# x of two groups fetched from DRAM by chunk instead of whole, in a fused attention and mixture-of-experts kernel

## The chip, the cores and the metric

The kernel runs on one core of a Trainium2 chip. The metric is the device time of one execution in microseconds; lower is better. The core has five engines with an instruction stream each, all in order: PE (matmul; its weight loads are shown apart, as PEld), DVE and ACT (elementwise), POOL, and SP, which here issues most of the DMA transfers. An engine whose next instruction waits for something holds up all that is queued behind it.

## The reference

A linear recurrence with a complex decay per channel gives y, and y, with the heads side by side, is the input x of a dense mixture of four experts:

```python
a_re_n, a_im_n = a * (min(mag, 0.999) / (mag + 1e-6))      # complex decay, 48 channels a head
for t in range(768):
    S = a_n[t] * S + k[t] (outer) v[t]                      # complex state, 48x48, 4x8 heads
    y[t] = q[t] @ real(S)
x = y.transpose(0, 2, 1, 3).reshape(3072, 384)
p = probs / (probs.sum(-1) + 1e-9)
out = sum over 4 experts e of  p[:, e] * (relu(x @ w1[e]) @ w2[e])     # w1 384x1024, w2 1024x384
```

## The kernel before

The 3072 rows are cut into 12 groups of G = 256 columns (tokens), each of two chunks of C = 128. For a group the attention part takes A, Q and K (prefix products and norms on DVE and ACT), sends Q and K to DRAM and back in another layout (trips `q_d`, `k_d` into `Qst`, `Kst`), and per chunk makes scores (`sc`), values (`yp`) and the increment of the state (`dp`) on PE. ACT evicts the values of a chunk into its half of the tile y.

The first two experts run beside the attention: while group g - 1 goes through `moe1` (16 slices of the hidden width, in 8 steps k of two), `between(k)` fits in the pieces of the attention of group g. A step multiplies x by a slice of w1 into `ph`; ACT makes hh = relu(ph) and DVE hl = relu(ph) - hh, and the matmuls of w2 on hh and hl go into `po` one step later. Each number is carried as a high and a low part, so x is split too: `split_x` makes xh, a copy by ACT in a reduced type, and xl = x - xh by DVE. Whenever an expert is done, ACT scales `po` into acc (L649), which frees the PSUM bank. Behind the 12 groups a second stage (phb, pob) runs the other two experts.

How x comes from y depends on the group. In groups 0 to 2 (`g < XSEL`) PE turns y of each chunk into the layout of x (`turn_x`), and `split_x` gets two parts. In groups 3 to 11 y goes to DRAM in two transfers (`store_y`, L623, one for each half of the partitions) once both chunks are evicted, and `load_x` (L159) fetches it whole into the tile x, of which there is one; L166 copies and L168 subtracts all 768 elements of each partition at once. The load has to wait on SP until the stores have landed. In `between` the three pieces of a group's attention are taken at three steps in a row from `FIRST` on (steps 4, 5, 6 for groups three and four), and `split_x` is called at step 7, the last one.

The order of instructions on an engine is not the order of the code: a planner writes it from simulated times, with the program's order as priority, except where `behind` or `tc.keep_in_program_order` fixes it. The latter sets an instruction behind the one traced before it on its engine; the copies and subtractions of `split_x` are so set.

Of the kernel before, what the change touches and what calls it, by code (L numbers as in the profile page):

```python
# [8 lines left out]
F32 = mybir.dt.float32  # L9
# [6 lines left out]
B, H, S, D = 4, 8, 768, 48  # L16
# [3 lines left out]
P = 128  # L20
NJ = HD // P
C = 128
G = 256
# [11 lines left out]
IM = 64  # L35
# [23 lines left out]
XSEL = 3  # L59
FIRST = {1: 5, 2: 5, 3: 4, 4: 4, 5: 3, 6: 3}  # L60
STEP = {1: 4.2, 2: 4.2, 3: 4.2, 4: 4.2, 5: 4.2}
MORE = (1.9, 1.9, 0.5)
HALF = (2, 3, 4, 5)
HOFF = 96
WIDE = 32 + P + 48
DMA_SCRATCH = 4096
# [2 lines left out]
def fast_path(ctx, tc, qkP, aP, vP, probsP, w, out, flag):  # L69
    nc = tc.nc  # L70
    const = ctx.enter_context(tc.tile_pool(name="const", bufs=1))
    wpool = ctx.enter_context(tc.tile_pool(name="wpool", bufs=NF1))
    moe = ctx.enter_context(tc.tile_pool(name="moe", bufs=2))
# [29 lines left out]
    y_d = [dram.tile([HD, G], F32, name=f"y_d{g}") for g in range(NG)]  # L103
# [50 lines left out]
        wts[i] = (hi, lo)  # L154
        return last_pe if ps is not None else None

    def load_x(g):
        x = moe.tile([P, NJ, G], F32, tag="x", name=f"xa{g}", bufs=1)
        nc.sync.dma_start(x, y_d[g].rearrange("(j p) t -> p j t", p=P))  # L159
        return [(slice(0, G), x)]  # L160

    def split_x(g, parts):
        xh = moe.tile([P, NJ, G], F32R, tag="xh", name=f"xha{g}")
# [65 lines left out]
    with ExitStack() as c1:  # L229
# [29 lines left out]
        nc.gpsimd.memset(TA, 0.0)  # L259
        band = moe.tile([M, HOFF + P + IM], F32, tag="x", name="band", bufs=1)  # L260
        nc.gpsimd.memset(band, 0.0)
        for r0, base in ((0, HOFF), (IM, HOFF + D)):
            nc.gpsimd.affine_select(out=band[r0:r0 + D], in_=band[r0:r0 + D], pattern=[[-1, HOFF + P + IM]],
                                    compare_op=ALU.not_equal, fill=1.0, base=base, channel_multiplier=1)
# [190 lines left out]
        def trip(nm, X, dst, lo=0, hi=CG, prev=None):  # L455
            w = X.shape[-1] if hi == CG else C
            dt = dram.tile([2, HD, hi - lo, w], F32, name=nm)
            for c in range(2):
                sent = nc.sync.dma_start(dt[c].rearrange("(j p) n t -> p j n t", p=P),
                                         X[:, c].rearrange("p (j n) t -> p j n t", n=CG)[:, :, lo:hi, :w])  # L460
                if prev is not None:
                    behind(sent, prev)

            def back(prev=None):
                for c in range(2):
                    landed = nc.sync.dma_start(dst[c * IM:c * IM + D, :, lo:hi, :w],
                                               dt[c].rearrange("(h d) n t -> d h n t", d=D))
                    if prev is not None:
                        behind(landed, prev)
                return landed  # L470
            back.sent = sent
            return back

        def t_factors(g):
            Tr, Ti = Qst[0:D, :, CG - 1, C:], Qst[IM:M, :, CG - 1, C:]
            ins = nc.scalar.activation(TA[0:D], Tr, AF.Copy)
            tc.keep_in_program_order(ins)
            behind(ins, state["y", g, CG - 1 if g < NSEL else 0])
            tc.keep_in_program_order(nc.scalar.activation(TA[IM:M], Tr, AF.Copy))
            tc.keep_in_program_order(nc.scalar.activation(TB[IM:M], Ti, AF.Copy))  # L480
            tc.keep_in_program_order(nc.scalar.activation(TB[0:D], Ti, AF.Copy, scale=-1.0))
# [80 lines left out]
        def rotate(g):  # L562
            if (g + 1) % GB == 0:
                return
            Gt = state[g, CG]

            def bt(ap):
                return ap.broadcast_to([ap.shape[0], H, D])

            nc.vector.tensor_tensor(P2[0:D], Gt[IM:M], bt(TB[IM:M]), op=ALU.mult)  # L570
            nc.vector.tensor_tensor(P2[IM:M], Gt[0:D], bt(TB[0:D]), op=ALU.mult)
            nc.vector.tensor_tensor(Gt, Gt, bt(TA), op=ALU.mult)
            state["dve"] = nc.vector.tensor_tensor(Gt, Gt, P2, op=ALU.add)
            state[g + 1, 0] = Gt

        def turn_x(g, c, y):
            xp = ps_a.tile([P, NJ, C], F32, tag="pa", name=f"xp{g}_{c}")
            for j in range(NJ):
                ps = [p for p in range(HP) if -HOFF < 2 * D * p - P * j < P]
                for p in ps:  # L580
                    o = HOFF - (2 * D * p - P * j)
                    state["xp"] = nc.tensor.matmul(xp[:, j, :], band[:, o:o + P], y[:, p, c * C:(c + 1) * C],  # L582
                                                   start=(p == ps[0]), stop=(p == ps[-1]))
            return slice(c * C, (c + 1) * C), xp

        def near_attention(g, QK):
# [26 lines left out]
            xs.append(turn_x(g, 1, y))  # L613
            yield xs
            store_y(g, y)
            t_factors(g)
            inc1()
            rotate(g)

        def store_y(g, y):  # L620
            yv = y_d[g].rearrange("(p u d) t -> u d p t", u=2, d=D)
            for u in range(2):
                nc.sync.dma_start(yv[u], y[u * IM:u * IM + D])  # L623

        def attention(g, QK):
            y = small.tile([M, HP, G], F32, tag="y", name=f"y{g}")
            (turn0, _, inc0, sc0, val0), (turn1, _, inc1, sc1, val1) = (chunk(g, c, QK[1], y) for c in range(CG))
            turn0()
            inc0()
            yield sc0()  # L630
            val0()
            t_factors(g)
            xs = [turn_x(g, 0, y)] if g < XSEL else None
            yield sc1()
            val1()
            if g < XSEL:
                xs.append(turn_x(g, 1, y))
            store_y(g, y)
            x = xs or load_x(g)
            turn1()  # L640
            inc1()
            rotate(g)
            yield x

        def moe1(g, xh, xl, between=None, prev=None):
            def done(e, po):
# [37 lines left out]
        def front(g, A, qk):  # L684
# [36 lines left out]
            yield 3.0  # L721
            if g in HALF:
                qb = [trip(f"q_d{g}_{c}", Q, Qst, c, c + 1) for c in range(CG)]
# [10 lines left out]
            else:  # L734
# [5 lines left out]
                qb()  # L740
                last["q"] = kb()
            todo[g] = attention(g, (Q, K))

        x = {}
# [345 lines left out]
```

## Time and profile before

| | us |
|---|---|
| median of 3 runs | 1008.11 (1007.4 to 1008.57) |
| the profiled execution | 1010.09 |
| its span in the trace | 1008.3 |
| PE busy | 981.6 (97%) |
| weight loads busy | 921.5 (91%) |
| DVE busy | 590.3 (59%) |
| ACT busy | 363.6 (36%) |
| POOL busy | 35.6 (4%) |

Busy times are sums over one profiled execution. PE is the engine that is nearly always busy; DVE and ACT are averages over a first part, to about 520 us, in which DVE is nearly as busy as PE, and a second part in which both do little. Matmul ends are modelled, so a short idle time of PE is better judged together with the waits of its weight loads. Group three's x is copied at 196.5 us, group four's at 244.8.

### The profile page before, as it was taken

The numbers are of one execution on the slowest core, as the hardware profiler recorded it, in microseconds if no ns is written. First come the engines' busy times: TensorE is split into PE (matmuls) and PEld (weight loads), VectorE is DVE, ScalarE is ACT, GpSimd is POOL, SyncE is SP. The second block draws the span as 40 slices with busy tenths as digits, with TensorE's granted clock in tenths as the row PEclk, the third lists the DMA queues.
The fourth block names the chain that finished last, engine by engine and source line by source line (L and its number), as shares of the span: only waits on it lengthen the run. The fifth ranks groups of instructions, "written<-read, shape, count | busy, mean of one in ns | idle before, by whom it ended". The sixth has DMA issues, their size and how long they took to land.

```text
span 1008.3 us, 16256 instructions
## 1 busy us (share of the span) xinstructions
PE 981.6 (97%) x6618; PEld 921.5 (91%) x6618; DVE 590.3 (59%) x1228; ACT 363.6 (36%) x652; POOL 35.6 (4%) x66
## 2 busy tenths in 40 slices
PE   5899999999999999999999999999999999999997
PEld 3899998999999999999999999999999899989996
DVE  7889989898987989798942462232132322321221
ACT  7755525446364453636422352121111211211110
POOL 6030000000000000000000000000000000000000
PEclk9899999999999999999999999999999999999999
DMA  9584277384673836548161780020030110100001
GB/s 311 162 177 134 64 189 156 119 204 110 166 191 111 225 108 160 157 119 213 60 162 46 252 297 33 1 94 32 1 126 1 42 52 1 63 1 1 32 1 35
DMA packets 88676, 111.15 MB, mean 110 GB/s; under 512 B 5840, under 2 KB 72960, under 8 KB 88592
## 3 DMA queue, kind: packets, MB, share of 16 engines
q1 hardware_dynamic: 84016, 94.11, 33.4%
q0 software_dynamic: 4576, 15.91, 5.2%
q8 instruction: 54, 0.88, 0.4%
q14 instruction: 30, 0.25, 0.1%
HBM read 74.09 MB, written 35.90 MB: 109 GB/s over the span
## 4 chain that ended last, share of the span: by engine, by line
PE 85%; DVE 4%; DMA 4%; ACT 4%; issue 1%; SPq 0%; DVEq 0%; ACTq 0%
PE pob L862 20%; PE phb L849 20%; PE po L198 16%; PE ph L179 16%; PE sc L530 4%; PE dp L518 3%; PE yp L551 2%; PE yp L546 2%; PE ktp L500 1%; DMA q_d<-Q 1%; DMA y_d<-y 1%; DMA Kst<-k_d 1%; DMA xa<-y_d 1%; PE xp L582 1%; DVE Q L430 1%
## 5 line engine op out<-in xcount | busy, mean ns | idle before, releaser
L855 DVE SCALAR_TENSOR_TENSOR hlb<-phb,hhb 128x512 fp32r<-128x512 f32 x96 | 66.4, 691 | 270.6 <-ACT hhb L854 270.6
L854 ACT ACTIVATE hhb<-phb 128x512 fp32r<-128x512 f32 x96 | 57.4, 598 | 314.9 <-PE phb L849 299.6
L198 PE MATMUL po<-whi,hh 128*128 128x384 f32 x384 | 129.6, 339 | 1.1 <-ACT hh L188 1.1
L862 PE MATMUL pob<-wlo,hhb 128*128 128x384 f32 x384 | 129.2, 337 | 0.0
L198 PE MATMUL po<-wlo,hh 128*128 128x384 f32 x384 | 128.9, 336 | 0.0
L862 PE MATMUL pob<-whi,hhb 128*128 128x384 f32 x384 | 128.9, 336 | 0.0
L198 PE MATMUL po<-whi,hl 128*128 128x384 f32 x384 | 124.5, 339 | 0.7 <-DVE hl L189 0.6
L862 PE MATMUL pob<-whi,hlb 128*128 128x384 f32 x384 | 120.4, 336 | 0.0
L188 ACT ACTIVATE hh<-ph 128x512 fp32r<-128x512 f32 x96 | 57.2, 596 | 153.3 <-PE ph L179 151.0
L179 PE MATMUL ph<-xha,whi 128*128 128x256 f32 x576 | 103.8, 286 | 0.6 <-ACT xha L166 0.6
L179 PE MATMUL ph<-xha,wlo 128*128 128x256 f32 x576 | 101.5, 283 | 0.0
L179 PE MATMUL ph<-xla,whi 128*128 128x256 f32 x576 | 100.8, 284 | 0.4 <-DVE xla L168 0.4
L189 DVE SCALAR_TENSOR_TENSOR hl<-ph,hh 128x512 fp32r<-128x512 f32 x96 | 66.1, 689 | 49.5 <-ACT hh L188 48.9
L849 PE MATMUL phb<-xhb,whi 128*128 128x512 f32 x288 | 91.8, 392 | 0.0
L179 PEld LDWEIGHTS ph<-xha,whi 128*128 128x128 f32 x576 | 86.0, 190 | 1.8 <-issue 0.9
L179 PEld LDWEIGHTS ph<-xla,whi 128*128 128x128 f32 x576 | 82.5, 191 | 0.6 <-DVE xla L168 0.6
L179 PEld LDWEIGHTS ph<-xha,wlo 128*128 128x128 f32 x576 | 82.8, 190 | 0.2 <-issue 0.2
L849 PE MATMUL phb<-xlb,whi 128*128 128x512 f32 x288 | 82.7, 392 | 0.0
L849 PE MATMUL phb<-xhb,wlo 128*128 128x512 f32 x288 | 82.3, 393 | 0.0
L862 PEld LDWEIGHTS pob<-whi,hhb 128*128 128x128 f32 x384 | 72.1, 188 | 3.6
L862 PEld LDWEIGHTS pob<-wlo,hhb 128*128 128x128 f32 x384 | 72.1, 188 | 3.3
L198 PEld LDWEIGHTS po<-whi,hh 128*128 128x128 f32 x384 | 72.4, 189 | 1.8 <-ACT hh L188 1.3
(165 smaller groups left out, 1569.2 us busy)
## 6 DMA issues: line engine op xcount, KB each, us to landing
wst<-w SPq DMA_DIRECT2D x24, 384.0 KB, 5.5
qk<-qkP SPq DMA_DIRECT2D x24, 384.0 KB, 7.0
acc_d<-acc POOLq DMA_DIRECT2D x24, 384.0 KB, 3.6
prev<-acc_d SPq DMA_DIRECT2D x24, 384.0 KB, 5.0
A<-aP SPq DMA_DIRECT2D x22, 384.0 KB, 8.0
q_d<-Q SPq DMA_DIRECT2D x12, 387.0 KB, 4.2
Qst<-q_d SPq DMA_DIRECT2D x12, 387.0 KB, 5.9
v<-vP SPq DMA_DIRECT2D x24, 192.0 KB, 2.7
```

The costliest lines, as they stand in the source:

```text
L179: ins = nc.tensor.matmul(ph[:, u, :], wt[:, j * P:(j + 1) * P], xt[:, j, :], start=(n == 0), stop=(n == 3 * NJ - 1))
L188: wts["hh"] = nc.scalar.activation(hh, ph, AF.Relu)
L189: nc.vector.scalar_tensor_tensor(hl, ph, 0.0, hh, op0=ALU.max, op1=ALU.subtract)
L198: nc.tensor.matmul(po[t], ht[:, u, t * P:(t + 1) * P], wt[:, HD:], start=(i % FE == 0 and n == 0), stop=(i % FE == FE - 1 and n == 2))
L518: nc.tensor.matmul(d_ps[:, h, :], KT[:, h, :], vc[:, h * D:(h + 1) * D], start=True, stop=True)
L530: ins = nc.tensor.matmul(s_ps[:, h, :], Kc[:, hf * 4 + h, :], Qc[:, hf * 4 + h, :], start=True, stop=True)
L546: ins = nc.tensor.matmul(yo, st[:, o:o + n], Qc[:, o // D, :], start=True, stop=False)
L551: ins = nc.tensor.matmul(yo, vc[:, o:o + n], sc[h // 4][:, h % 4, :], start=first, stop=True)
L849: nc.tensor.matmul(ph, wt[:, j * P:(j + 1) * P], xt[:, j, :], start=(n == 0), stop=(n == 3 * NJ - 1))
L854: nc.scalar.activation(hh, ph, AF.Relu)
L855: nc.vector.scalar_tensor_tensor(hl, ph, 0.0, hh, op0=ALU.max, op1=ALU.subtract)
L862: ins = nc.tensor.matmul(po[t], ht[:, t * P:(t + 1) * P], wt[:, HD:], start=(i % FE == 0 and n == 0), stop=(i % FE == FE - 1 and n == 2))
```

## The change

In groups three and four (`XHALF`) y of chunk 0 is sent to DRAM right after its own eviction, and x of chunk 0 is loaded behind that, ahead of the scores of chunk 1; y of chunk 1 follows with a second pair of stores and a second load into the same tile. `split_x` then gets two parts and makes two copies and two subtractions of half the size. Groups 5 to 11 stay as they are.

```diff
+XHALF = (3, 4)
...
-    def load_x(g):
-        x = moe.tile([P, NJ, G], F32, tag="x", name=f"xa{g}", bufs=1)
-        nc.sync.dma_start(x, y_d[g].rearrange("(j p) t -> p j t", p=P))
-        return [(slice(0, G), x)]
+    def load_x(g, ts=slice(0, G), x=None):
+        if x is None:
+            x = moe.tile([P, NJ, G], F32, tag="x", name=f"xa{g}", bufs=1)
+        nc.sync.dma_start(x[:, :, ts], y_d[g].rearrange("(j p) t -> p j t", p=P)[:, :, ts])
+        return [(ts, x[:, :, ts])], x
...
-        def store_y(g, y):
+        def store_y(g, y, ts=slice(0, G)):
             yv = y_d[g].rearrange("(p u d) t -> u d p t", u=2, d=D)
             for u in range(2):
-                nc.sync.dma_start(yv[u], y[u * IM:u * IM + D])
+                nc.sync.dma_start(yv[u][:, :, ts], y[u * IM:u * IM + D, :, ts])
...
             t_factors(g)
-            xs = [turn_x(g, 0, y)] if g < XSEL else None
+            xs, x = [turn_x(g, 0, y)] if g < XSEL else [], None
+            if g in XHALF:
+                store_y(g, y, slice(0, C))
+                xs, x = load_x(g, slice(0, C))
             yield sc1()
             val1()
             if g < XSEL:
                 xs.append(turn_x(g, 1, y))
-            store_y(g, y)
-            x = xs or load_x(g)
+            rest = slice(C, G) if g in XHALF else slice(0, G)
+            store_y(g, y, rest)
+            if g >= XSEL:
+                xs = xs + load_x(g, rest, x)[0]
             turn1()
             inc1()
             rotate(g)
-            yield x
+            yield xs
```

## Rows read from the trace of the kernel before

**Rows 1.** The page, part 1: busy us (share of the span), instructions.

```profile
PE 981.6 (97%) x6618; PEld 921.5 (91%) x6618; DVE 590.3 (59%) x1228; ACT 363.6 (36%) x652; POOL 35.6 (4%) x66
```

**Rows 2.** Waits of PE from 262 us: who for whom, total us, times, longest.

```profile
PE sc L530 <- DMA Kst<-k_d: 0.8, 1, 0.8
```

**Rows 3.** Stretches: length, busy PE, PEld, DVE, ACT, POOL (instructions), PE clock, DMA share, GB/s.

```profile
196.00:206.00 10.00, 9.77 (x68) 9.12 (x66) 8.54 (x17) 7.93 (x14) 0.00 (x0) 1.00 0.34 92
206.00:216.00 10.00, 9.68 (x69) 9.64 (x70) 9.83 (x16) 5.76 (x10) 0.54 (x1) 1.00 0.91 225
...
246.00:256.00 10.00, 9.94 (x71) 9.56 (x70) 8.65 (x16) 6.73 (x11) 0.54 (x1) 1.00 0.49 124
```

**Rows 4.** Waits of all engines, 186 to 206 us.

```profile
ACT xha L166 <- DMA xa<-y_d: 2.7, 1, 2.7
DVE xla L168 <- ACT xha L166: 2.2, 1, 2.2
...
PEld po L198 <- DVE hl L189: 0.4, 1, 0.4
```

**Rows 5.** Waits of all engines, 206 to 216 us.

```profile
PEld po L198 <- DVE hl L189: 0.8, 1, 0.8
```

**Rows 6.** The chain that ended last, 186 to 206: start us, us, what.

```profile
189.17 4.07 DMA y_d<-y
...
193.29 3.19 DMA xa<-y_d
...
205.67 0.61 DVE hl L189
```

**Rows 7.** Waits of all engines, 236 to 256 us.

```profile
ACT xha L166 <- DMA xa<-y_d: 1.8, 1, 1.8
...
ACT u L334 <- DMA q_d<-Q: 1.6, 1, 1.6
...
PEld po L198 <- ACT acc L649: 0.4, 2, 0.3
```

**Rows 8.** Lines L166 and L168: ns min/median/max, first and last start, shapes.

```profile
L166 ACT ACTIVATE xha<-xa x9: 832/846/847, 196.5 to 558.3; 128x768 fp32r<-128x768 f32 x9
L166 ACT ACTIVATE xha<-xp x6: 484/491/536, 47.1 to 152.7; 128x384 fp32r<-128x384 f32 x6
...
L168 DVE TENSOR_TENSOR xla<-xa,xha x9: 949/958/960, 197.4 to 559.2; 128x768 fp32r<-128x768 f32 x9
L168 DVE TENSOR_TENSOR xla<-xp,xha x6: 550/553/558, 50.1 to 154.8; 128x384 fp32r<-128x384 f32 x6
```

**Rows 9.** DMA issues: transfer, count, KB each, median us to landing.

```profile
q_d<-Q SPq DMA_DIRECT2D x12, 387.0 KB, 4.2
...
Kst<-k_d SPq DMA_DIRECT2D x12, 384.0 KB, 6.2
...
Kst<-k_d SPq DMA_DIRECT2D x16, 192.0 KB, 4.6
...
q_d<-Q SPq DMA_DIRECT2D x10, 192.0 KB, 3.5
```

**Rows 10.** Line L623, 180 to 290 us: issue ns min/median/max on SP.

```profile
L623 SPq DMA_DIRECT2D y_d<-y x6: 325/326/326, 188.6 to 279.4; - x6
```

**Rows 11.** Timeline of ACT: start, us, line, shapes, idle before: evictions of y.

```profile
180.63 1.20 ACT L558 ACTIVATE y<-yp 48x512 f32<-48x512 f32 x2 [1.27 <-PE yp L551]
...
187.94 1.21 ACT L558 ACTIVATE y<-yp 48x512 f32<-48x512 f32 x2 [3.42 <-PE yp L551]
...
228.78 1.20 ACT L558 ACTIVATE y<-yp 48x512 f32<-48x512 f32 x2 [3.02 <-PE yp L551]
...
235.53 1.21 ACT L558 ACTIVATE y<-yp 48x512 f32<-48x512 f32 x2 [3.40 <-PE yp L551]
```

**Rows 12.** Timeline of SP and PE: Kst and first scores of group five.

```profile
257.36 2.06 SPq L466 DMA_DIRECT2D Kst<-k_d  x2
...
263.29 2.02 PE L530 MATMUL sc<-Qst,Kst 112*128 112x128 f32 x16
```

## The prediction

> **What bounds the kernel now.** I read the page first: PE is busy for 981.6 of 1008.3 us [rows 1], so only 26.7 us of the whole span is not matmul. A change that adds and takes away no matmul can therefore win only what PE loses by waiting around groups three and four, or what it loses later for their sake. So the next view is the stretches of 10 us around the two places where x is copied and subtracted (about 196 us for group three, 245 us for group four). In 196 to 206 PE is busy 9.77 of 10 us, in 206 to 216 it is 9.68, in 246 to 256 it is 9.94 [rows 3]: 0.23, 0.32 and 0.06 us idle, 0.61 in all. Matmul ends are modelled, so I take the weight loads as the other reading of the same loss. They show a wait of 0.4 us on DVE's hl before 206 and one of 0.8 us after it [rows 4, 5], and two waits in group four, 0.4 us in all, on ACT's acc, which must empty the PSUM bank [rows 7]. PE's loss is thus between 0.55 and 1.2 us in group three and between 0.06 and 0.4 us in group four. No matmul waits for x itself in either group; the only wait of any length after them is one of 0.8 us for Kst near 306 us, ahead of group six [rows 2].
>
> **Where the waits of group three come from.** The chain that ended last, in the window 186 to 206, names it: the last eviction of y ends at 189.17, the store of y to DRAM takes 4.07 us to land, the load of x another 3.19, and after the copy and the subtraction DVE works without a break up to the hl at 205.67 that PE waits for [rows 6]. ACT stood 2.7 us before the copy and DVE 2.2 us before the subtraction [rows 4]. Both engines run in order, so all that is queued behind (rotate, the squares, Q, the hl) is late by that. That is the wait that the change attacks: PE does not wait for x but for a DVE that waited for x. In group four ACT stands 1.8 us before the copy, but soon afterwards another 1.6 us for the store of Q to land (tmp buffers are reused), and only then comes the acc that PE wants [rows 7]. Ending the first of these stalls lengthens the second.
>
> **Part 1, the trip of chunk 1.** After the change the last trip carries half the bytes. Store: two transfers of 96 instead of 192 KB; load: 192 instead of 384 KB. The trace has no trip of that size in y and x, but other tensors go both ways whole and by chunk: q_d stores 387 KB in 4.2 and 192 KB in 3.5 us, Kst loads 384 KB in 6.2 and 192 KB in 4.6 us [rows 9], savings of 17% and 26%. Applied to 4.07 and 3.19 us that is 0.7 + 0.8 = 1.5 us. Bounds: nothing saved at the one end; at the other the load and the store save as much as the Kst rows do in us, 1.6 each, 3.2 together. I take 1.5, as these rows have the same short runs of 128 columns. The Trainium skill, "DMA: Bandwidth & Descriptors", section "Anatomy of one DMA — SWDGE (gpsimd) path", speaks against this: it gives about 2.0 us per transfer that do not depend on size, plus bytes over 436 GB/s. An estimate by that page is 0.45 us saved on the load and 0.22 on the store, 0.7 us in place of 1.5; the trace's 3.19 us for 384 KB [rows 6] is near the 2.9 that the page's numbers give, so the trace does not contradict it, and by it the first rival below has less to overcome.
>
> **Part 2, copy and subtraction by chunk.** One copy of 128x768 takes 846 ns and one of 128x384 takes 491, the subtractions 958 and 553 [rows 8] (the halves read PSUM there and SBUF here; I take them as they are). Behind the landing stand then 0.49 + 0.55 instead of 0.85 + 0.96: 0.77 us less. Chunk 0 has landed by then. Added work: 2 x 491 - 846 = 136 ns of ACT and 2 x 553 - 958 = 148 ns of DVE per group. In group three both are hidden in the 2.7 and 2.2 us in which the engines stood; were that cover gone, DVE's order up to the hl would lengthen by 0.15 us, less than the shortest of the two waits. In group four ACT has its 1.8 us, DVE has no wait of its own there and pays 0.15 us away from PE's path.
>
> So xl of group three is ready 1.5 + 0.77 = 2.3 us earlier (0.77 to 4.0 by the bounds), and all of DVE's order behind it can move up by as much, until it meets another wait. The waits need 0.4 and 0.8. Both go even near the lower bound.
>
> **Part 3, the extra trip of chunk 0.** Per group two stores and one load more on SP: three issues of about 0.33 us [rows 10], 1.0 us, and a wait on SP in the middle, as the load must see its store landed. Group three: chunk 0 is evicted from 180.63 to 181.83 [rows 11]; with the 4.07 us of the whole store the load is issued near 185.9 and has landed near 189.1. Chunk 1 begins its eviction at 187.94, so its first store could go at about 188.5: SP is free by then, by some 2 us. Group four: evicted by 229.98, load near 234.1, chunk 1's first store near 236.1 [rows 11]: 2 us again. What is queued behind SP's wait is chunk 1's store, and the loads of v that come due there are small and early; the K and Q trips come after the second load in either order. I cost this at nothing, hidden in SP's idle time. If the store of chunk 1 had to wait until chunk 0's load had landed (both use the same y_d tensor), it would cost about 0.6 us in group three (189.1 against 188.5) and 1.2 in group four.
>
> **The sum.** Group three gives back its waits: between 0.55 (PE idle) and 1.2 (weight loads), I take the middle, 0.9. Group four: 0 to 0.4; I take 0, as the landing of Q's store releases ACT there, and chunk 1's lighter load beside it may at best bring that forward a little. Part 3: 0. Total 0.9 us. The profiled execution took 1010.09 us, 1008.3 of it span, and would take 1009.2. It lies 2.0 us above the median of the three runs, 1008.11, and I carry the difference over to the median: 1007.2 us. A measurement of this kernel can tell about 0.2%, or 2.0 us, from no change, so this counts as the same.
>
> **Rivals.**
> First, the gain is eaten: chunk 1's trip is hardly shorter, or its store is held behind chunk 0's load, or the orders that the planner writes anew from its simulated times put the second subtraction where DVE waits as long as now. For it: the planner set the subtraction at a place where DVE stands 2.2 us before it [rows 4], so its times for x are not the chip's. Against it: the copies alone give 0.77 us. A hold of 0.6 us with nothing saved in flight leaves xl 0.17 us earlier, which cures neither wait fully. Time 1008.1, from 1007.9 to 1009.
>
> Second, slower: a stall moved into the path of K. The copy of chunk 0 is pinned only behind one earlier ACT instruction; if the planner puts it, or the second copy, ahead of ACT work that feeds K and it waits there for its load, the K trip slips. That costs nothing where the trip has slack, and a us per us where it has none. Group five's first scores are such a place: Kst is issued from 257.36, over 2.06 us, and lands some 4.6 us behind its issue, near 263 to 264; the scores start at 263.29 [rows 9, 12]. The price is a stall of the size seen in these groups, 2.7 us [rows 4], with no stall removed ahead of it: 1008.1 + 2.7 = 1010.8. It decides from about 2 us of new delay on. Against it: chunk 0's load lands 6 to 7 us ahead of the present time of the copy.
>
> Third, much faster: with x early the new order also clears the waits that follow. All there is: 1.2 + 0.4 + 0.8 us [rows 2, 4, 5, 7] = 2.4, time 1005.7. Nothing links the wait on Kst at 306 us to x of groups three or four, so this needs luck.
>
> **How the numbers follow.** Forecast 0.63, first rival 0.21, second 0.11, third 0.05. The forecast and the first rival lie within 0.2% (1006.1 to 1010.1): same 0.84; slower 0.11; faster 0.05. The range: the forecast's own bounds are 0.55 to 1.6 us of gain, 1006.5 to 1007.6; measured medians wander by some tenths (the three runs reach from 1007.4 to 1008.57), which lowers the end to 1006.2; upward it takes in the first rival and what a new order may cost in small waits, to 1009.4. The two outer rivals, 0.16 together, are left out.
>
> **What would show it.** Right: in 185 to 197 us two loads of x, the second landing near 195; ACT's and DVE's waits before the second copy shorter by a us or more; no wait of the weight loads on hl in 196 to 210; PE busy 10.0 of 10 in both stretches; the start of group six's scores about 0.9 us earlier. Wrong: a store of chunk 1 that leaves SP only after chunk 0's load has landed (first rival); a new wait on Kst near 263 us or a longer one near 306 (second); PE gaps at new places in later groups, where no x is split, which would mean that the planner's order moved more than the transfers did.

## The result, and the profile after

The changed kernel takes 1010.15 us (median of 15 executions, 1008.78 to 1011.7) against 1008.11 us for the kernel before on the same chip (15 executions, 1006.65 to 1009.12): ratio 1.0015, 95% interval 1.0009 to 1.0022. The ratio is still within the 0.2% that was called the same, but the forecast of 1007.2 us had the sign wrong, and the time lies outside its range. On two more chips the ratio was 1.0008 (0.9999 to 1.0016) and 1.0012 (1.0002 to 1.0021), so the usual loss is about 1 us, and 2 us on the first chip. Medians are over all executions; the ratios leave out four disturbed ones (1630 to 2498 us, two of them of the run after_2).

The profiled execution of after took 1009.96 us, 1008.3 of it span. The first row is part 1 of its page (busy us, share, instructions). PE is as busy as before within 2 us [rows 1]:

```profile
PE 979.7 (97%) x6618; PEld 920.4 (91%) x6618; DVE 589.7 (58%) x1230; ACT 363.8 (36%) x654; POOL 35.7 (4%) x66
```

SP's timeline of group three (start, us, engine, line, transfer) shows the change doing what it says. Chunk 0 is stored at 180.55 and loaded at 184.00, long before chunk 1's store at 187.86, and that store follows its eviction at once: nothing holds it back.

```profile
180.55 1.36 SPq L625 DMA_DIRECT2D y_d<-y  x2
184.00 0.38 SPq L161 DMA_DIRECT2D xa<-y_d  x1
187.86 0.92 SPq L625 DMA_DIRECT2D y_d<-y  x2
191.62 0.38 SPq L161 DMA_DIRECT2D xa<-y_d  x1
```

The chain that ended last in 186 to 206 us (start, us, what) gives chunk 1's trip: 3.07 + 2.33 = 5.40 us, where the whole trip took 4.07 + 3.19 = 7.26 [rows 6].

```profile
188.48 3.07 DMA y_d<-y
...
191.62 2.33 DMA xa<-y_d
```

So x is early. But DVE's timeline (start, us, line, shapes, idle before) shows what DVE does with the time it got:

```profile
194.53 0.56 DVE L170 TENSOR_TENSOR xla<-xa,xha 128x384 fp32r<-128x384 f32 x1 [1.06 <-ACT xha L168]
...
198.23 1.83 DVE L432 TENSOR_TENSOR Q<-A,qk 128x768 f32<-128x768 f32 x2
199.97 0.55 DVE L574 TENSOR_TENSOR G<-G,TA 112x384 f32<-112x384 f32 x1
200.44 0.95 DVE L326 CUSTOM_DVE_ANT_0 s<-s 128x768 f32<-128x768 f32 x1
201.32 0.08 DVE L326 DVE_READ_ACCUMULATOR2_ANT st_m<- 128x1 f32 x1
201.32 0.69 DVE L191 SCALAR_TENSOR_TENSOR hl<-ph,hh 128x512 fp32r<-128x512 f32 x1
```

Q of group four (1.83 us) and the sum of squares of group five (0.95 us) now stand ahead of the hl that PE wants. In the kernel before both stood behind it. Counted from the first eviction (179.93 and 180.63 us), x was ready 2.6 us later there, and hl still began 1.1 us earlier:

```profile
200.96 0.68 DVE L189 SCALAR_TENSOR_TENSOR hl<-ph,hh 128x512 fp32r<-128x512 f32 x1
201.56 1.82 DVE L430 TENSOR_TENSOR Q<-A,qk 128x768 f32<-128x768 f32 x2
...
203.76 0.95 DVE L324 CUSTOM_DVE_ANT_0 s<-s 128x768 f32<-128x768 f32 x1
```

The waits of 186 to 206 us (engine, line, for whom: us, times, longest) show the price: one wait for hl of 1.1 us on PE, 1.5 on the weight loads, where the weight loads of before had 0.4 and, a little later, 0.8 [rows 4, 5].

```profile
ACT xha L168 <- DMA xa<-y_d: 2.6, 1, 2.6
...
PEld po L200 <- DVE hl L191: 1.5, 1, 1.5
PE po L200 <- DVE hl L191: 1.1, 1, 1.1
```

And the stretches (length, busy PE, PEld, DVE, ACT, POOL, PE clock, DMA share, GB/s) answer to [rows 3]: the second and third are now full, as forecast, but the first has lost nearly 1 us of PE (8.85 against 9.77).

```profile
196.00:206.00 10.00, 8.85 (x63) 8.53 (x63) 9.80 (x20) 6.37 (x11) 0.00 (x0) 1.00 0.45 100
206.00:216.00 10.00, 10.00 (x72) 9.78 (x71) 8.04 (x11) 6.17 (x12) 0.54 (x1) 1.00 0.80 192
246.00:256.00 10.00, 10.00 (x75) 10.00 (x75) 9.09 (x17) 5.67 (x9) 0.54 (x1) 1.00 0.41 116
```

A second trace of the kernel before (same_before below) has 9.27 in the first, and its other two are as good as full without the change. So the full stretches here are no sign of a gain, in group four above all:

```profile
206.00:216.00 10.00, 9.93 (x70) 9.89 (x71) 9.83 (x16) 5.50 (x9) 0.54 (x1) 1.00 0.89 220
246.00:256.00 10.00, 10.00 (x75) 10.00 (x74) 9.13 (x18) 6.56 (x11) 0.54 (x1) 1.00 0.48 132
```

PE's waits from 262 us on are two of 0.4 us, one for hl in group eight and one for Kst near 348 us; the one of 0.8 near 306 [rows 2] is absent.

```profile
PE po L200 <- DVE hl L191: 0.4, 1, 0.4
PE sc L532 <- DMA Kst<-k_d: 0.4, 1, 0.4
```

So groups three and four explain why nothing was gained. They do not yet explain a loss of 1 us.

### The profile page after: what moved, and what is told of

Its sections match the earlier page's. It is cut to its first block, busy times and chain, and to the rows that moved or that the text cites. A ratio compares the mean times of both kernels' runs of the same rounds, so it can differ in the third digit from the quotient of the medians.

```text
span 1008.3 us, 16266 instructions
## 1 busy us (share of the span) xinstructions
PE 979.7 (97%) x6618; PEld 920.4 (91%) x6618; DVE 589.7 (58%) x1230; ACT 363.8 (36%) x654; POOL 35.7 (4%) x66
## 4 chain that ended last, share of the span: by engine, by line
PE 87%; DVE 4%; ACT 3%; DMA 2%; issue 1%; DVEq 0%; ACTq 0%; SPq 0%
PE pob L869 20%; PE phb L856 20%; PE po L200 17%; PE ph L181 17%; PE sc L532 4%; PE dp L520 3%; PE yp L553 2%; PE yp L548 2%; PE ktp L502 1%; DMA y_d<-y 1%; DMA Kst<-k_d 1%; DMA xa<-y_d 1%; PE xp L584 1%; PE qp L392 0%; ACT y L560 0%
```

## The experiments

The theories are that the new order costs time (O), that the loss lies in the start or the end (S, then R and R2), that each added trip costs (T), that the later groups are hurt (N, L). Every time is set against executions of the kernel before on the same chip. Two quantities are read from all traces, beside the times. **Group three's stretch** is the time from the last eviction of y of group three to that of group four. **The end** is the span less the moment at which the last DVE operation ends.

### The same two kernels again, and each group alone

The edits of the third and the fourth run are `XHALF = (3,)` and `XHALF = (4,)`; the first two are the kernels before and after, unchanged.

> The kernel before, unchanged, as a second sample of its trace: the profile of before lies 2.0 us above the median of its runs, and its PE clock was at 0.60 between 24 and 32 us. Every theory expects 1008.1 us, ratio 1.000 within 0.001. If the excess of that one profile came from its start, the marks up to 180 us lie some 0.5 to 2 us earlier here, and the marks behind 180 us keep their distances.

> The changed kernel, unchanged, as a second sample. Theory O (the new order of PE and DVE in group three costs time): ratio 1.0015 to 1.002, with the loss between 176 and 260 us of the trace. Theory S (nothing is lost between 176 and 600 us, the difference lies in the start or in the tail, ahead of group three or behind the last matmul): the same ratio, but the stretch from group three's first eviction (about 180 us) to the last matmul is no longer than before.

> XHALF = (3,): only group three goes by chunk. PE's order is then that of the change in full. Theory O: the whole loss, ratio 1.0015 to 1.002. Theory T (each chunked trip costs by its extra transfers): half of it, 1.0008. Theory S: as the change in full, if the loss comes with the program and not with the stretch.

> XHALF = (4,): only group four goes by chunk. PE's order is then that of the kernel before. Theory O: no loss, 1.000 within 0.0005. Theory T: half of it, 1.0008. The recorded forecast of nothing gained in group four: 1.000.

Measured against 1008.03 us: same_before 1007.63 (0.9996, 0.9987 to 1.0005), same_after 1008.88 (1.0008, 0.9999 to 1.0016), only_g3 1008.41 (1.0005, 0.9997 to 1.0014), only_g4 1007.34 (0.9995, 0.9986 to 1.0004). Neither half alone shows the 1 us (only_g3's interval still reaches it), and two loads of one program differ by 0.4 us. The traces say why details must not be read from one execution: same_before's span is 1005.8 us, 2.5 less than the profiled execution that I forecast from, and the wait for Kst near 306 us [rows 2] is absent in it. Group three's stretch is 47.85 us in same_before, 47.59 in before, 47.82 in after, 47.52 in same_after and 47.69 in only_g3: nothing won, nothing lost. The end is 6.7 and 6.3 us in the two traces of before, 6.1 and 6.5 in the two halves, but 7.5 and 7.7 in the two of after. In SP's part of the trace there is one thing that sets these two apart: SP has 541 entries (semaphore steps included), against 532 in before, 536 in only_g3 and 537 in only_g4.

### hl first, and a first try at SP's list

hl_first takes group five's squares, on ACT and on DVE, behind the last hh and hl of the block beside group three's trip. `late` moves 12 us (by the kernel's own estimates) of the preparation of later groups, which `advance` issues, from the last step of that block to the first of the next. In the trace PE's order changes too, near 206 to 208 us. SP's list stays.

```diff
+                if g == 5:
+                    for x, p in zip(ins + [sq], (wts["hh"], wts["hl"], wts["hh"])):
+                        behind(x, p)
...
-        nc.vector.scalar_tensor_tensor(hl, ph, 0.0, hh, op0=ALU.max, op1=ALU.subtract)
+        wts["hl"] = nc.vector.scalar_tensor_tensor(hl, ph, 0.0, hh, op0=ALU.max, op1=ALU.subtract)
...
+                late = {(3, nk - 1): -12.0, (4, 0): 12.0}.get((g, k), 0.0)
-                advance(STEP.get(g, 3.4) + (MORE[k - first] if first <= k <= end else 0.0), g + 1)
+                advance(STEP.get(g, 3.4) + (MORE[k - first] if first <= k <= end else 0.0) + late, g + 1)
```

pad9 lengthens the list of the kernel before (`PAD = 9`), lean9 shortens that of the changed one (`LEAN = 9`), lean_hl is lean9 with hl first:

```diff
-                    nc.sync.dma_start(prev[e][:, u * CG:(u + 1) * CG, :], acc_d[R2 * r + u][e])
+                    for t in range(CG) if r * E1 * R2 + e * R2 + u < PAD else (slice(0, CG),):
+                        nc.sync.dma_start(prev[e][:, u * CG:(u + 1) * CG, :][:, t], acc_d[R2 * r + u][e][:, t])
```

```diff
-                    nc.sync.dma_start(prev[e][:, u * CG:(u + 1) * CG, :], acc_d[R2 * r + u][e])
+                    (nc.gpsimd if r * E1 * R2 + e * R2 + u < LEAN else nc.sync).dma_start(
+                        prev[e][:, u * CG:(u + 1) * CG, :], acc_d[R2 * r + u][e])
```

> The kernel before, with nothing of the change, but nine of stage two's loads of the kept sums (prev) issued as two halves each, so that SP has 9 instructions more before its last branch, as the changed kernel has (515 in the trace of after, 506 before). They land some hundred us before they are read. Theory R (the end runs longer because SP has more instructions): the time from the last DVE operation to the end of the span goes from 6.3-6.7 us to 7.5 us or more, and the kernel takes 1.0 to 1.4 us longer than before, about 1009.3. Theory N (the loss lies in groups three and four, and the long end of two profiles is chance): end 6.3-6.7 us, time as before, 1008.1 within 0.4.

> The changed kernel, but nine of the loads of the kept sums (prev) in stage two are issued from GpSimd instead of SP, so that SP has as many instructions before its last branch as before the change. Groups three and four are left as changed. Theory R: the end takes 6.3-6.7 us again and the kernel about 1.2 us less than the changed one, about 1008.2. Theory N: the end may vary, the time stays with the changed kernel, 1009.5 within 0.5.

> The changed kernel, but the sums of squares of group five (ACT squares L324 and L325, DVE L326) are issued behind the last hh and hl of the block that runs when group three's x comes back; the work itself is the same, only its place in the order of ACT and DVE changes between 198 and 260 us, SP's list does not. Theory O2 (hl stands 0.95 us later than it need in the new order, and PE waits for it): PE's wait for hl near 202 us goes from 1.15 us to about 0.3 and the stretch to group four's first eviction is 0.6 to 0.8 us shorter; kernel 1008.8. Theory G (the wait moves to the next hl, whose ACT and DVE lists are as full): the stretch stays within 0.3 us and so does the time, 1009.5. The end stays long (7.5 us) by theory R.

> Both of the last two edits: SP's list as short as before the change, and the last hl ahead of group five's squares. R and O2 together: end 6.3-6.7 us, group three 0.6 to 0.8 us shorter, kernel 1007.4, which is 0.7 below the kernel before. R with G: 1008.2. N with O2: 1008.8. N with G: 1009.5.

Measured against 1007.24 us: pad9 1008.86 (1.0013, 1.0004 to 1.0022), lean9 1011.0 (1.004, 1.0028 to 1.0052), hl_first 1008.1 (1.0009, 1.0 to 1.0018), lean_hl 1011.02 (1.0031, 1.002 to 1.0043).

The order theory holds for group three. DVE's timeline of hl_first has hl ahead of the squares:

```profile
198.15 1.83 DVE L435 TENSOR_TENSOR Q<-A,qk 128x768 f32<-128x768 f32 x2
199.89 0.55 DVE L577 TENSOR_TENSOR G<-G,TA 112x384 f32<-112x384 f32 x1
200.36 0.68 DVE L191 SCALAR_TENSOR_TENSOR hl<-ph,hh 128x512 fp32r<-128x512 f32 x1
...
201.89 0.95 DVE L326 CUSTOM_DVE_ANT_0 s<-s 128x768 f32<-128x768 f32 x1
```

Its waits and its stretch follow: 0.3 us in place of 1.1, PE at 9.72 in place of 8.85, and group three's stretch is 46.64 us.

```profile
PE po L200 <- DVE hl L191: 0.3, 1, 0.3
```

```profile
196.00:206.00 10.00, 9.72 (x68) 9.40 (x67) 9.92 (x21) 8.00 (x15) 0.54 (x1) 1.00 0.46 113
```

Over all traces of this study PE waits for hl in 196 to 216 us for 0.4 to 1.0 us with the order of before (seven traces, mean 0.6), 1.1 to 1.3 with that of the change (six, mean 1.2), and 0.2 to 1.1 with hl first (seven, mean 0.6). The stretch has means of 47.69, 47.68 and 46.93 us. So with the change's order nothing is left of what the early x could save; with the order that has hl first it is 0.75 us (46.5 to 47.4 against 47.4 to 48.0 in the traces of the order of before).

On SP's list the first try was half a miss. pad9 costs time as expected, with an end of 6.8 us where 7.5 was expected. Its order in stage two changed with it, at no cost in its trace. But lean9 and lean_hl moved loads at the start of stage two, and with them the order there: from group eleven's last eviction to the sixth eviction of stage two they take 77.1 and 77.2 us against 74.3, so their times decide nothing. Their ends, 5.7 and 6.7 us, are short.

### Group eight, where the trip binds

after and same_after lost 0.4 to 1.1 us, against before's two traces, between the last evictions of groups eight and nine, where all orders are equal. That stretch follows the moment at which ACT starts to copy group eight's x. The rows are ACT's timeline of same_after: 14.17 us from the eviction to the copy.

```profile
411.83 1.19 ACT L560 ACTIVATE y<-yp 48x512 f32<-48x512 f32 x2
...
426.00 0.85 ACT L168 ACTIVATE xha<-xa 128x768 fp32r<-128x768 f32 x1 [5.23 <-DMA xa<-y_d]
```

| trace | eviction to copy, us | stretch of group eight, us |
|---|---|---|
| pad9 | 12.81 | 42.97 |
| same_before | 13.04 | 43.18 |
| hl_first | 13.07 | 43.21 |
| before | 13.42 | 43.55 |
| after | 13.80 | 43.92 |
| same_after | 14.17 | 44.31 |

Each us of a late x is a us of PE here, down to about 12.8 us. SP's timeline of same_after says why x is late: SP stands in order, and the store of y (415.99) is listed behind the load of Qst (415.58), which waits for q_d to land. So the store leaves 4.2 us after the start of the eviction, where that takes 1.2; in same_before it leaves after 3.5, and the rest of the difference between the two lies in how long store and load took to land.

```profile
411.04 0.96 SPq L461 DMA_DIRECT2D q_d<-Q  x2
415.58 0.32 SPq L468 DMA_DIRECT2D Qst<-q_d  x1
415.99 0.91 SPq L625 DMA_DIRECT2D y_d<-y  x2
...
422.22 0.38 SPq L161 DMA_DIRECT2D xa<-y_d  x1
```

Hence after once more, hl_first once more, the change in group eight alone (x8, `XHALF = (8,)`), and hl_first with `XHALF = (3, 4, 8)` (x348hl).

> The changed kernel once more, loaded anew, beside the three below. Its two traces so far lost, against the traces of the kernel before, 0.6 to 1.1 us between the last evictions of y of groups eight and nine (43.92 and 44.31 us against 42.97 to 43.57), where the order of the work is the same in both kernels, and nothing clear in groups three and four. There the first copy of group eight's x starts 13.80 and 14.17 us after the eviction, against 12.81 to 13.42, behind a wait for its load. Theory L (this lateness belongs to the changed kernel): again 13.6 us or more and 43.8 or more; time 1.0 to 1.5 us over before. Theory C (it belongs to one load of a program or to chance): 12.2 to 13.5 and 43.0 to 43.6 us; time 0.3 to 1.0 over before.

> The changed kernel with group five's squares behind the last hh and hl of the block beside group three's trip, once more, now timed on one chip with the changed kernel. O2: the stretch between the last evictions of y of groups three and four is 46.6 us again (47.5 to 47.8 in the changed kernel) and the time 0.8 to 1.1 us below that of the changed kernel; against before 0 to +0.5. If the gain of group three is given back later: time equal to the changed kernel's within 0.4.

> The change made in group eight alone (groups three and four as before): the order of all other work on every engine is that of the kernel before. Group eight is where the traces show PE bound by x's return: the stretch to group nine's last eviction follows the moment at which x's copy starts one for one (43.21 us at 13.07, 43.55 at 13.42, 44.31 at 14.17) and is 42.96 where it is early enough. Theory B (the trip is worth what it shortens a bound stretch by): second copy starts at 11.5 us or less, the stretch is 42.9 to 43.0, time 0.2 to 0.6 us below before. Rival T (the added store and load cost elsewhere, as the two added in groups three and four did): time 0.3 to 0.7 over before.

> hl_first with group eight's trip by chunk as well. O2 and B together: stretch of group three 46.6 us, that of group eight 42.9 to 43.0, time 0.2 to 0.6 us below hl_first_2 and 0.5 to 1.3 below before. T: 0.3 to 0.7 over hl_first_2.

Measured against 1007.74 us: after_2 1008.83 (1.0012, 1.0002 to 1.0021), hl_first_2 1008.27 (1.0004, 0.9995 to 1.0013), x8 1007.39 (0.9998, 0.9989 to 1.0006), x348hl 1007.84 (1.0003, 0.9994 to 1.0012). Two forecasts were missed: hl_first_2's stretch is 47.1 us and not 46.6 (its time, 0.56 us below after_2 by the medians and 0.8 by the ratios, just about meets the 0.8 to 1.1), and x348hl came out level with before where 0.5 to 1.3 below was expected. after_2's copy in group eight starts after 13.22 us and the stretch is 43.37: the lateness of the two earlier traces belonged to their executions, not to the change (C), yet the time is 1 us over before all the same. In x8 the second copy starts after 11.64 us:

```profile
412.71 1.19 ACT L560 ACTIVATE y<-yp 48x512 f32<-48x512 f32 x2
...
424.35 0.53 ACT L168 ACTIVATE xha<-xa 128x384 fp32r<-128x384 f32 x1 [2.28 <-DMA xa<-y_d]
```

Its stretch is 42.97 us, the floor, and so it is in every later trace with group eight by chunk. The trip does what was hoped for where it binds, for 0.2 to 1.3 us; the time, 0.35 us below before, agrees but is within its interval. The ends: 7.0 us in after_2, 6.9 in hl_first_2, 7.1 in x348hl, 6.0 in x8, whose SP has 536 entries.

### SP's list and nothing else

pad_late and lean_late repeat pad9 and lean9 with the last nine loads of the kept sums (`LATE = range(15, 24)` in place of the first nine): pad_late issues them in halves, lean_late from GpSimd. PE, DVE and ACT keep their orders to the last instruction. lean_before is the control of lean_late, best is x348hl with the last twelve loads on GpSimd.

```diff
+LATE = range(15, 24)
...
-                    nc.sync.dma_start(prev[e][:, u * CG:(u + 1) * CG, :], acc_d[R2 * r + u][e])
+                    (nc.gpsimd if (r * E1 + e) * R2 + u in LATE else nc.sync).dma_start(
+                        prev[e][:, u * CG:(u + 1) * CG, :], acc_d[R2 * r + u][e])
```

> The kernel before with nine SP instructions more, as pad9, but the nine loads of kept sums that are issued in halves are the last nine of stage two, so that the order of work on PE, DVE and ACT is that of the kernel before throughout. Theory R2 (the end of the span is longer by some 0.5 to 1.2 us where SP has 541 instructions or more in the trace: 6.8 to 7.7 us in the seven such traces so far, 5.8 to 6.7 us in the seven with 537 or fewer): end 6.8 us or more, time 0.5 to 1.2 us over before. Theory P (pad9's 1.3 us came from the loads it split at the start of stage two): end may vary, time as before within 0.4.

> The changed kernel with the last nine loads of kept sums in stage two issued from GpSimd, so that SP has fewer instructions than it had before the change; the order on PE, DVE and ACT is that of the changed kernel throughout (the nine of lean9 stood at the start of stage two and cost about 3 us there). R2: end 5.8 to 6.7 us, time 0.5 to 1.2 us below the changed kernel, which is that of before within 0.4. P: time stays 0.8 to 1.4 us over before.

> The control: the kernel before with the last nine loads of kept sums issued from GpSimd. R2 with a step between 537 and 541 instructions: end 5.8 to 6.7 us and time as before, within 0.4. If the end grows with every instruction: 0.5 us or more below before. If the issue from GpSimd itself gains or costs, this shows it: lean_late is then to be read against this run.

> hl_first with group eight by chunk as well (x348hl) and the last twelve loads of kept sums issued from GpSimd. If group three's order (0.75 us), group eight's trip (0.3 us) and the end (R2, 0.5 to 1.2 us) add up: end 5.8 to 6.7 us, time 0.6 to 1.3 us below before. If the end is not the cause: 0 to 0.4 over before, as x348hl was.

Measured against 1007.83 us: pad_late 1008.6 (1.0007, 0.9998 to 1.0016), lean_late 1008.2 (1.0005, 0.9996 to 1.0014), lean_before 1008.22 (1.0006, 0.9997 to 1.0015), best 1007.12 (0.9992, 0.9983 to 1.0001). Last came best again and x38hl, which is hl_first with `XHALF = (3, 8)`:

> The version that came out 0.7 to 0.8 us below the kernel before, once more on another load, to see whether its lead holds: 0.4 to 1.2 us below before if it does; within 0.3 of before if it was chance.

> The trip by chunk in groups three and eight only (group four as before, where PE did not wait for x in any trace), with hl ahead of group five's squares, and all loads of kept sums on SP. SP has 540 instructions or so in the trace, between the 537 with a short end and the 541 with a long one. Group three 46.6 to 47.2 us, group eight 42.9 to 43.0. With a short end (under 6.7 us): 0.7 to 1.1 us below before. With a long one: 0 to 0.4 below.

Measured against 1007.97 us: best_2 1007.18 (0.9997, 0.9988 to 1.0006), x38hl 1008.68 (1.0011, 1.0002 to 1.002).

The end can be read from DVE's last row (start, us) and the span above it; the four operations end 2.19 us after their start. First the kernel before (same_before), 1005.8 - 997.32 - 2.19 = 6.3 us:

```profile
core 0 of [0], span 1005.8 us
...
997.32 2.19 DVE L873 SCALAR_TENSOR_TENSOR prev<-pob,pr,prev 128x384 f32<-128x384 f32 x4 [1.28 <-PE pob L862]
```

The same rows of after, 7.6 by them (7.5 in finer numbers):

```profile
core 0 of [0], span 1008.3 us
...
998.54 2.19 DVE L880 SCALAR_TENSOR_TENSOR prev<-pob,pr,prev 128x384 f32<-128x384 f32 x4 [1.28 <-PE pob L869]
```

Of pad_late, 7.1, which is the kernel before but for SP's list:

```profile
core 0 of [0], span 1007.1 us
...
997.84 2.19 DVE L874 SCALAR_TENSOR_TENSOR prev<-pob,pr,prev 128x384 f32<-128x384 f32 x4 [1.28 <-PE pob L863]
```

Of best, 6.3:

```profile
core 0 of [0], span 1005.8 us
...
997.29 2.19 DVE L885 SCALAR_TENSOR_TENSOR prev<-pob,pr,prev 128x384 f32<-128x384 f32 x4 [1.28 <-PE pob L874]
```

All twenty traces of the case fall apart in two sets without overlap: SP with 537 entries or fewer, end 5.7 to 6.7 us (eleven traces, mean 6.3); SP with 540 or more, end 6.8 to 7.7 us (nine, mean 7.2). x38hl, with 540, is among the long ones (7.3). It looks like a step between 537 and 540 and not a slope: lean_before, with 515, has 6.6.

SP's own steps at the end stand in no view, but the traces have their times, and they part the end at the landing of the last store of out. That store lands 2.95 to 5.05 us behind DVE's last operation, with means of 4.3 and 4.4 us in the two sets: no difference. What follows takes 2.07 us in both traces of before and 2.68 in all three of after (1.7 to 2.8 in all short ends, 2.4 to 3.2 in the long ones). In each of the nine long ends SP stands still for 0.36 to 0.88 us ahead of its 536th entry, whichever step that is; in pad_late it is 0.51. Lists of 536 entries end there, and in only_g4 (537) a pause of 0.68 falls on SP's last steps, where the other traces have a wait of about 0.5 anyway. So 0.6 us of after's longer end comes with SP's list, and the rest of the 0.9 is how late the last store landed in those executions.

The times agree, within intervals of about 0.9 us to either side. The kernel before with the longer list takes 0.77 us more (pad_late, whose interval just includes 1; pad9's does not), the changed kernel 0.85 to 1.1 on two chips. Without the end, the traces of the two kernels are level: 1001.7 and 999.5 us in before, 1000.7, 1000.9 and 999.2 in after. With the shorter list, the changed kernel (lean_late) and the kernel before (lean_before) differ by 0.02 us. Both lie 0.4 us over before, which I read as the price of GpSimd's issues, though it is inside both intervals. At either length of the list the change itself is worth nothing that these runs can tell.

## Why the prediction was wrong, step by step

**What bounds the kernel, and where group three's waits come from: right.** PE does not wait for x there but for DVE's hl; with the order of hl_first, where hl stands ahead of the squares, the early x is worth 0.75 us.

**Part 1: right, and a little low.** I took 1.5 us for chunk 1's shorter trip; the rows give 7.26 - 5.40 = 1.86. The estimate of 0.7 us by the Trainium skill, "DMA: Bandwidth & Descriptors", section "Anatomy of one DMA — SWDGE (gpsimd) path", is not borne out by these transfers: 1.86 us was saved. That fit is for transfers that GpSimd issues; these are issued by SP.

**Part 2: right.** xl of group three is ready at 195.09, which is 15.16 us after the first eviction (179.93); before it was 17.72 us, as the subtraction of [rows 8] begins near 197.4 and the eviction of [rows 11] at 180.63. That is 2.56 us earlier where 2.3 was forecast.

**Part 3: right in its place, wrong in the sum.** SP is idle where the trip is added, and chunk 1's store is not held. The term "I cost this at nothing" failed all the same, 800 us later: SP's nine further entries (six transfers and their semaphore steps) take its list over a step, and the end of the span grows by 0.9 us (means 7.2 against 6.3), of which the traces tie 0.6 to the list.

**"All of DVE's order behind it can move up by as much": this step failed.** DVE's order did not move up, it was written anew, and Q and the squares went ahead of hl. Of the 0.9 us nothing was left. The first rival named the planner's new order, but looked for the harm in the second subtraction, which came early; it had a chance of 0.21 and, at 1008.1, a time without loss. With the 0.6 to 0.9 us of the end in the sum, that rival comes to 1008.7 to 1009.0 us, near where two of the three chips have it (0.85 and 1.1 us over before).

**The second rival,** a stall in K's path, did not come: there is no new Kst wait near 263 us, none near 306, and the one of 0.4 us near 348 is shorter than the 0.8 of [rows 2]. **The third** needed luck, and had none.

**The base.** I forecast from one execution that took 2 us more than the median and carried the difference over. same_before shows that such an execution has waits of its own (Kst, 306 us) which the next has not. This moved no term of the sum, but single waits of 0.3 to 0.8 us, on which my 0.9 rested, are no firmer than that: PE's wait for hl alone ranges from 0.4 to 1.0 us over seven traces with one and the same order.

**What stays open.** The first chip shows 2.0 us where the others show about 1. x38hl, by group three, group eight and the end, should be level with before, and took 0.7 us more, so stretches read from one trace each add up to the times only to within about 0.7 us. best came out 0.7 and 0.8 us below before on two chips by the medians (0.8 and 0.3 by the ratios), with both intervals reaching 1: perhaps ahead of both kernels, not shown. Why SP pauses ahead of its 536th entry is open too.

## What to carry to other kernels

Where a planner writes the orders, an operand that comes earlier is not yet a wait that ends earlier: look up which instruction the bottleneck waits for, and pin that one ahead of what may take its place. Shorten a transfer where the bottleneck's stretch follows it one for one (group eight here), not where an engine off the path stands the longest before it. And count the instructions that a change adds even on an idle queue: lengthen the list alone, without the change, to see what they cost.

## What the runs showed of the hardware

**The end of the program depends on the length of SP's list.** With 540 entries or more the nine traces have a pause of SP of 0.36 to 0.88 us ahead of the 536th, behind the last store; pad_late, which lengthens the list and nothing else, has it (0.51 us), and lean_late, which shortens that of the changed kernel, has not (end 5.9 us).

The jump over unused code is not what sets the two sets apart. In the kernel as it stands, DVE, ACT and SP jump over a second, general path after the last store; from SP's jump to its next step it is 2.7 to 3.2 us in sixteen traces and 3.4 to 4.0 in four (three of after, and x38hl at 3.86). In these four that step waits for the last store, which lands 0.02 us earlier. The Trainium skill, "Runtime: NRT & Kernel Launch", section "Instruction fetch mechanics", says that a taken branch to a place outside the fetched window makes the engine wait for a fetch. That fits the 2.7 us and more that every trace spends there, whatever its end. From 1001 us on after fetches instructions (queue, kind: packets, MB, share of 16 engines), and so does same_before, whose end is short:

```profile
q14 instruction: 5, 0.04, 1.8%
q8 instruction: 1, 0.02, 1.3%
```

```profile
q14 instruction: 5, 0.04, 1.8%
q8 instruction: 1, 0.02, 1.1%
```

Whether the pause ahead of the 536th entry is a wait for a fetch is not shown.

**A transfer of half the size took about a quarter less than the whole:** 3.07 against 4.07 us for the store of y, 2.33 against 3.19 for the load of x.

**One and the same list of transfers differs by up to 1 us between executions.** Group eight's copy of x started 13.2, 13.8 and 14.2 us after the eviction in the three traces of after, and 12.2 to 14.2 us in the fifteen traces that do not split it; by the table above PE pays what exceeds 12.8.
